# Attention and a gated spatial MLP on one core: three intermediate steps change engine and memory, and the instruction order is replaced

## The chip, the cores and the metric

The kernel runs on one core of one Trainium2 chip. A core has five engines that run at once and wait for each other through semaphores: TensorE (PE, matrix products, written to PSUM), VectorE (DVE), ScalarE (ACT), GpSimd (POOL) and SyncE (SP, here the queue of nearly all DMAs). The metric is the device time of one execution in microseconds, less is better. The time before is 403.96 us, the median of three runs (400.94 to 404.26).

## What is computed

Four batches of 768 tokens. Attention with eight heads of 64, in which a token sees the first four tokens and the last 128 up to itself; its result feeds an MLP whose gate mixes tokens.

```python
scores = q @ k^T / sqrt(64)                 # (4, 8, 768, 768), only sinks and window kept
a = softmax(scores);  x = a @ v             # (4, 768, 512): heads side by side
h = relu(x @ w_in)                          # (4, 768, 1024), split into u and v of 512 each
v_n = (v - mean(v)) / sqrt(var(v) + 1e-6)   # over the 512 of a token
v_s = einsum('ts,bsd->btd', w_spatial, v_n) + b_spatial[t]
out = (u * v_s) @ w_out                     # (4, 768, 512)
```

All inputs are float32 (w_in and w_out arrive as float64 words that are decoded on the chip). The products run in float16 with each operand split into a high and a low half, and three products for a pair (high by high, high by low, low by high).

## The kernel before, in words

The work is cut into pieces, each a Python closure of one to some tens of instructions on one engine: `plan.add` registers about 1900 of them with a rank, an engine (or several that may take it), what they read and what they write. The ranks number the pieces; the costs have no effect on a written-out order. The order in which they are issued is the list `ORDER` (L273): numbers of pieces, with a letter behind a number where the engine is chosen (a ScalarE, d VectorE, p GpSimd). Every engine runs its own pieces in that order and waits at each for what it needs, so the list fixes all queues, SyncE's DMA queue among them. 24 short pieces of idle products (`keep_clock`) are registered, and six of them are in the list, near the start.

A batch has six tiles of 128 tokens, and a tile two halves of four heads: an attention step is one half of a tile, 48 in all (step 20 is batch 1, tile 4, first half). For a step the stages are: scores on TensorE (`scores`, L880 for batch 0 in float32, L886 after it); mask and row minimum on VectorE (L891); exponential on ScalarE (L896); the probabilities p split into a high half (L536 or L545) and a low half (L552), each transposed by a DMA from SyncE (L961); products with v into the tile's attention sum `av` (`attend`, L993 to L1012). `av` has one buffer, of two PSUM banks, and is written by both steps of a tile.

Behind the second step of a tile the sum is divided (`divide`, L1019 to L1023, VectorE) into the SBUF tile `x`, which is split into `x16`: a high half on ScalarE or GpSimd, a low half on GpSimd (the helpers `high`, L536 to L545, and `low`, L552, record one line for all tiles). A DMA transposes `x16` into `xT`.

`v_half` computes v for a tile: product into `ps_v`, relu (L1063, ScalarE), statistics (`stats`, L1069 to L1073, VectorE: bn_stats, bn_aggr, then a scaling of the variance), its power of -1/2 (`root`, L1079, GpSimd), normalisation (L1087, VectorE), and the halves of `vn`. `u_half` computes u for two tiles and 128 of its columns (relu at L1112). When all six `vn` of a batch are there, `s_piece` forms the spatial product for 256 tokens and 128 columns into `ps_s` (18 matmuls); `gate` (L1133, VectorE) adds the bias and writes the sum into the SBUF tile `g`; `times` (L1137, VectorE or GpSimd as the list says) multiplies it with u; halves of `g` follow. `o_piece` multiplies with w_out (12 matmuls), copies (L1159, ScalarE) and stores.

`ps_v`, `ps_u`, `ps_s`, `ps_o` and the transposed blocks of batch 0's first tiles share two PSUM banks ("mm") in turn, so a product waits until the last but one before it has been read out. Scores have four banks.

Weights are loaded and decoded by the same engines in the first 120 us or so, beside batch 0. Near the end checks decide whether a general path must run (`KNOWN`, the place in the list where every engine reads the decision).

Of the kernel before, what the change touches and what calls it, by code (L numbers as in the profile page):

```python
# [269 lines left out]
KNOWN = 1874  # L270
ORDER = """
165 1892 1898 1894 1 0 3 37 116 164 68 5 42 39 4 44 43 1891 1893 2 62 6 40 41 13 38 15 63 11 51 50 14 46 16 45 47 64 48 73 65 17 49 74 66 20 19 21 18
1886 52 67a 10 69 71 88 82 70 7 112 9 111 85 22 87 75 86 25 91 8 93 104 108 107 26 89a 92 101 100 27 12 57 102 84 110 31 105 53 123 103 132 128 129 32  # L273
109 28 126 127 114a 141 106 156 115a 33 34 140 130 113 142 29 151 144a 143 54 150 133 229 172 124p 162 61 90 146 131 145a 159 158 148 76 147 161 77
139 72 163 35 160 152 169a 78 117 30 55 183 36 94 153 157 184 173 95 182 154 170d 188 224 223 125 179 263 83 221 209 194 178 190 191 155 196a 58 168
171 59 192 205 186 185 193 215 187 166 206 79 135 174p 199 222 410 201 96 149 230 198 228 218 210 197a 220 175 23 217 200 167 232 207a 189 216 211 24
212d 219 244 225 243 233 119 231 204 257 208 319 226 213 259 239 134 118 250 97 245a 240 80 261 251 120 227 252d 98 234a 176 345 56 177 235 180 247
267 236 60 99 121 181 136 260 258 283 346 275 248 270 271 262 253 195 122 286 344 289 202p 285 276 81 203p 294 284 313 288 279 287 277a 237 304 305
274 297 137 306a 293 280 281d 138 343 387 214 278 309 310 315 311d 299 300 316 295a 298 327 351a 291 317 318 423 379 328 337 282 321 432 296 446 352
331 389 339 290 329p 322 349 307 340 292 371 341 353 354 372 301 323 342 308 314 312 350 375 326 333d 332 373a 347 338 416 355 334 362 480 417 426  # L280
# [54 lines left out]
class Plan:  # L335
# [945 lines left out]
```

## Time and profile before

| | before |
|---|---|
| time, median of three runs | 403.96 us (400.94 to 404.26) |
| profiled execution, its own time | 402.65 us |
| its span, first to last instruction | 400.8 us |
| busy TensorE / VectorE / ScalarE / GpSimd | 384.4 / 319.7 / 282.7 / 206.1 us |
| HBM read / written | 38.17 / 6.29 MB |

The profile is of one execution. Busy times are from the first cycle of an instruction to its end; matmuls overlap, and their ends are modelled, so a group's busy time over its count is the better price of one than its mean. A view by form groups instructions of one line, engine, operation and shape: total busy us and mean ns, then the idle time of the engine just before them and what ended it. A timeline has one instruction or a run of equal ones to a line.

### The profile page before, as it was taken

What the parts mean: (1) busy time and instruction counts of PE and PEld (TensorE: products, weight loads), DVE (VectorE), ACT (ScalarE), POOL (GpSimd) and SP (SyncE); (2) the same over time, 40 slices, a digit from 0 to 9 for tenths busy, and PEclk for the clock granted to TensorE, in tenths of its full rate; (3) what the DMA queues carried; (4) which work ended last, traced back from release to release, by engine and by line L of the source; (5) the groups of instructions that cost most, each with busy time, mean ns of one, the idle gap of its engine ahead of it and who ended that gap; (6) DMA issues with size and microseconds to landing.
All of it is one profiled execution on the core that took longest, in us unless ns stands there. A gap on an engine that the chain in (4) does not pass through costs nothing. (4 is left out here: it accounts for less than half of the span.)

```text
span 400.8 us, 10029 instructions
## 1 busy us (share of the span) xinstructions
PE 384.4 (96%) x3663; PEld 270.1 (67%) x3663; DVE 319.7 (80%) x898; ACT 282.7 (71%) x681; POOL 206.1 (51%) x265
## 2 busy tenths in 40 slices
PE   7999999989998998999999999998999999999995
PEld 5775587558854774668785785586778666587842
DVE  4999999999999988889998987899679864545310
ACT  4998799979989887879889778896485433322011
POOL 5456545836873766463675674474375642232500
PEclk9999899999999999999999999999999999999999
DMA  8999799778889998797969996988838894123012
GB/s 272 335 352 222 201 196 211 217 199 235 135 208 208 225 216 160 222 240 179 218 165 155 229 219 156 232 176 191 143 79 167 197 196 111 54 80 105 2 56 109
DMA packets 134872, 72.91 MB, mean 182 GB/s; under 512 B 114208, under 2 KB 118304, under 8 KB 134816
## 3 DMA queue, kind: packets, MB, share of 16 engines
q1 hardware_dynamic: 134400, 71.94, 77.7%
q8 instruction: 30, 0.49, 0.5%
q10 hardware_dynamic: 416, 0.26, 0.2%
q14 instruction: 26, 0.21, 0.2%
HBM read 38.17 MB, written 6.29 MB: 111 GB/s over the span
## 5 line engine op out<-in xcount | busy, mean ns | idle before, releaser
L573 PE MATMUL ps_s<-wsp,vn 128*128 128x256 f16 x864 | 99.3, 273 | 2.4 <-ACT u L1112 1.4
L896 ACT ACTIVATE pexp<-pexp,nm 128x260 f32<-128x260 f32 (+1 forms) x192 | 86.2, 486 | 14.6 <-DVE nm L891 14.2
L573 PEld LDWEIGHTS <-vn 128*128 128x128 f16 x864 | 83.2, 98 | 15.2 <-issue 4.7
L573 PE MATMUL ps_u<-xT,win 128*128 128x256 f16 x576 | 69.2, 273 | 2.2 <-DVE nm L891 1.3
L573 PE MATMUL ps_v<-win,xT 128*128 128x512 f16 x288 | 66.3, 380 | 0.3 <-DMA xT<-x 0.3
L573 PE MATMUL ps_o<-wout,g 128*128 128x512 f16 x288 | 65.1, 379 | 0.8 <-DVE g L1133 0.8
L573 PEld LDWEIGHTS <-win 128*128 128x128 f16 x576 | 54.7, 98 | 12.8 <-issue 2.9
L552 DVE TENSOR_TENSOR p<-pexp,p 128x16 f16<-128x16 f32 (+2 forms) x62 | 52.0, 848 | 0.2 <-ACT p L536 0.2
L573 PEld LDWEIGHTS <-xT 128*128 128x128 f16 x288 | 27.2, 98 | 32.4 <-issue 2.2
L573 PEld LDWEIGHTS <-g 128*128 128x128 f16 x288 | 27.9, 98 | 31.4 <-issue 1.2
L536 ACT CAST p<-pexp 128x32 f16<-128x32 f32 (+2 forms) x62 | 36.9, 611 | 1.8 <-DMA pT<-p 1.0
L1159 ACT ACTIVATE ob<-ps_o 128x512 f32<-128x512 f32 x24 | 14.2, 591 | 34.0 <-PE ps_o L573 31.8
L552 POOL TENSOR_TENSOR x<-x,x 128x512 f16<-128x512 f32 x24 | 30.0, 1252 | 10.8 <-ACT x L536 10.1
L1133 DVE SCALAR_TENSOR_TENSOR g<-ps_s,b_bc 128x256 f32<-128x256 f32 x48 | 20.1, 420 | 18.0 <-PE ps_s L573 17.5
L1137 POOL TENSOR_TENSOR g<-g,u 128x256 f32<-128x256 f32 x25 | 23.8, 954 | 20.2 <-DVE g L1133 19.1
L999 PE MATMUL av<-vring,pT 128*128 128x65 f16 x312 | 33.2, 195 | 0.3 <-DMA pT<-p 0.3
L1000 PE MATMUL av<-vring,pT 128*128 128x65 f16 x312 | 33.0, 194 | 0.0
L1001 PE MATMUL av<-vring,pT 128*128 128x65 f16 x312 | 32.9, 194 | 0.0
L1079 POOL TENSOR_TENSOR rs<-rs,mhalf 128x1 f32<-128x1 f32 x24 | 18.2, 761 | 26.1 <-DVE rs L1073 25.9
L999 PEld LDWEIGHTS <-pT 128*128 128x128 f16 x312 | 29.0, 98 | 3.0 <-DMA pT<-p 1.0
L1112 ACT ACTIVATE u<-ps_u 128x256 f32<-128x256 f32 x48 | 17.9, 374 | 16.4 <-PE ps_u L573 16.2
L1000 PEld LDWEIGHTS <-pT 128*128 128x128 f16 x312 | 28.9, 98 | 0.8 <-DVE vring L559 0.2
(154 smaller groups left out, 758.1 us busy)
## 6 DMA issues: line engine op xcount, KB each, us to landing
qkraw<-qk_t SPq DMA_DIRECT2D x18, 512.0 KB, 4.3
out<-ob SPq DMA_DIRECT2D x24, 256.0 KB, 3.2
vraw<-v_s SPq DMA_DIRECT2D x21, 256.0 KB, 3.9
dec<-w_in SPq DMA_DIRECT2D x8, 512.0 KB, 6.9
wrow<-w_in SPq DMA_DIRECT2D x8, 512.0 KB, 3.9
wrow<-w_sp_rows SPq DMA_DIRECT2D x6, 384.0 KB, 3.9
dec<-w_out SPq DMA_DIRECT2D x4, 512.0 KB, 4.8
wrow<-w_out SPq DMA_DIRECT2D x4, 512.0 KB, 4.0
```

Source lines behind the costliest of these rows:

```text
L536: nc.scalar.copy(o, x)
L552: eng[e].tensor_tensor(out=o, in0=x, in1=hi, op=ALU.subtract)
L573: nc.tensor.matmul(o, a, m, start=(i == 0), stop=(i == n - 1))
L896: nc.scalar.activation(po, po, AF.Exp, bias=nm()[:, h2 + q:h2 + q + 1], scale=-1.0)
L999: nc.tensor.matmul(o[:, h], ph, vh, start=(t < 2 and j == 0), stop=False)
L1000: nc.tensor.matmul(o[:, h], ph, vl, start=False, stop=False)
L1001: nc.tensor.matmul(o[:, h], pl, vh, start=False, stop=(j == nb - 1 and (t < 2 or h == HH - 1)))
L1079: nc.gpsimd.tensor_tensor(out=vals["rs", i], in0=vals["rs", i], in1=mhalf, op=ALU.pow)
L1112: plan.add(r + WHEN["u relu"], "a", 0.37, lambda e: nc.scalar.activation(tl("u", (b, c0))[:, d, :], tl("ps_u", i)[:, :TC], AF.Relu, scale= ...
L1133: nc.vector.scalar_tensor_tensor(out=g(), in0=tl("ps_s", i)[:, :TC], scalar=1.0 / (SP_SCALE * VNS), in1=b_bc[:, t0:t0 + TC], op0=ALU.mult, ...
L1137: eng[e].tensor_tensor(out=g(), in0=g(), in1=tl("u", (b, c0))[:, d, :], op=ALU.mult)
L1159: plan.add(r + WHEN["o copy"], "a", 0.5, lambda e: nc.scalar.activation(tl("ob", i), tl("ps_o", i), AF.Copy, scale=1.0 / (G_SCALE * OUT_SC ...
```

## The change

Three edits and a new list. (1) `divide` writes its quotient back over the attention sum in PSUM; the SBUF tile `x` is gone. The high half of x is taken from there on ScalarE or VectorE and the low half on VectorE (GpSimd before). (2) `gate` writes its sum back over `ps_s` where the product is done on VectorE, which then reads it from PSUM; where GpSimd does the product, the sum still goes to `g`. (3) The scaling of the variance moves from VectorE to GpSimd, ahead of the power. (4) `ORDER` holds the same 1892 pieces (six idle ones among them) in another order and with other engines: on VectorE 35 gate products (before 23), 19 low halves of p (before 32), 8 low halves of vn (13); on ScalarE 24 high halves of p (32), 20 of x (9), 29 of g (21), 4 of k (9); on GpSimd 23 low halves of p (10), 18 high halves of p (10), 14 of k (9), 16 low halves of vn (11). The remaining changed lines are costs, which have no effect on a written-out order, and bookkeeping (`where` tells `gate` which engine has the product). Of the list, some lines are shown.

```diff
@@ -228,8 +228,8 @@
 
 ENGINES = {
     "w_in high": "a", "w_sp high": "a", "v high": "a", "q high": "a", "k high": "ap", "p high": "ap",
-    "sink high": "a", "x high": "ap", "vn high": "adp", "g high": "ap", "q low": "dp", "k low": "dp",
-    "p low": "dp", "sink low": "d", "x low": "p", "vn low": "dp", "g low": "dp", "v relu": "a", "normalise": "d",
+    "sink high": "a", "x high": "ad", "vn high": "adp", "g high": "ap", "q low": "dp", "k low": "dp",
+    "p low": "dp", "sink low": "d", "x low": "d", "vn low": "dp", "g low": "dp", "v relu": "a", "normalise": "d",
     "gate": "dp", "w clamp": "d", "w_out low": "p", "pT copy": "ad",
 }
 BANKS = {"sc": 4, "av": 1, "mm": 2}
@@ -267,67 +267,67 @@
-KNOWN = 1874
+KNOWN = 1881
 ORDER = """
-165 1892 1898 1894 1 0 3 37 116 164 68 5 42 39 4 44 43 1891 1893 2 62 6 40 41 13 38 15 63 11 51 50 14 46 16 45 47 64 48 73 65 17 49 74 66 20 19 21 18
-1886 52 67a 10 69 71 88 82 70 7 112 9 111 85 22 87 75 86 25 91 8 93 104 108 107 26 89a 92 101 100 27 12 57 102 84 110 31 105 53 123 103 132 128 129 32
-109 28 126 127 114a 141 106 156 115a 33 34 140 130 113 142 29 151 144a 143 54 150 133 229 172 124p 162 61 90 146 131 145a 159 158 148 76 147 161 77
...
-1794p 1871 1872d 1833 1873p 1874p 1795 1834p 1835p 1796 1836d 1797d 1852 1853 1881 1883 1857 1861 1858 1862 1863 1885 1880 1882 1884 1864 1798p 1799d
-1810 1815 1817 1811 1816 1818
+5 0 1895 1 3 2 4 1908 6 11 1898 10 53 1889 7 164 1894 9 14 13 8 42 39 15 44 16 43 51 41 40 50 62 46 47 45 63 37 1887 64 17 112 48 52 116 38 111 73 19
+229 74 12 65 49 68 105 67a 21 72 20 18 69 83 66 82 22 387 54 71 75 70 88 86 91 55 85 87 25 26 104 89d 100 84 172 163 101 107 162 23 92 103 61 93 128
+106 31 319 110 263 109 108 246 27 32 123 90 129 113 102 28 57 115a 132 459 114a 127 131 209 165 126 124a 194 141 156 142 140 143 33 130 29 146 125 34
...
+1836d 1793a 1794d 1758 1883 1885 1795 1763 1851 1807 1796 1797d 1798p 1799d 1880 1808 1809p 1812p 1852 1882 1853 1813d 1884 1811 1810 1816 1857 1815
+1817 1818 1858 1861 1863 1862 1864
 """.split()
@@ -340,10 +340,11 @@
 
 
     def __init__(self, rings, ring_of):
-        self.pieces, self.rings, self.ring_of = [], rings, ring_of
+        self.pieces, self.rings, self.ring_of, self.where = [], rings, ring_of, {}
 
     def add(self, rank, engines, time, f, reads=(), writes=(), dma=None, shared=False, columns=0, alone=True):
         self.pieces.append((rank, len(self.pieces), engines, time, f, tuple(reads), tuple(writes), dma, shared, columns, alone))
+        return len(self.pieces) - 1
 
     def prepare(self):
         ps = self.ps = sorted(self.pieces, key=lambda x: x[:2])
@@ -366,9 +367,11 @@
 
     def order(self):
         self.prepare()
-        for x in ORDER:
-            p = self.ps[int(x.rstrip("adp"))]
-            yield p[4], x[-1] if x[-1] in "adp" else p[2]
+        todo = [(self.ps[int(x.rstrip("adp"))], x[-1]) for x in ORDER]
+        todo = [(p, e if e in "adp" else p[2]) for p, e in todo]
+        self.where = {p[1]: e for p, e in todo}
+        for p, e in todo:
+            yield p[4], e
 
 
 class Begin:
@@ -494,7 +497,6 @@
             "pexp": ("pexp", sb([P, HH, 2, SEG], F32, "pexp", PEB)),
             "p16": ("p16", next_p16),
             "pT": ("pT", sb([P, 4 * HH + 2, P], F16, "pT", PTB)),
-            "x": ("x", sb([P, 2, HH, D], F32, "x", 1)),
             "x16": ("x16", sb([P, 2, 4 * P], F16, "x16", 2)),
             "xT": ("xT", sb([P, 2, KC, TC], F16, "xT", XTB)),
             "g": ("g", sb([P, TC], F32, "g", GB)),
@@ -1020,7 +1022,7 @@
                 else:
                     nc.vector.tensor_scalar(den, o[:, :, :, D], 1e-9, None, op0=ALU.add)
                 nc.vector.reciprocal(den, den)
-                nc.vector.tensor_tensor(out=tl("x", (b, t)), in0=o[:, :, :, :D],
+                nc.vector.tensor_tensor(out=o[:, :, :, :D], in0=o[:, :, :, :D],
                                         in1=den.unsqueeze(3).to_broadcast([P, 2, HH, D]), op=ALU.mult)
             if whole_av(b, t):
                 plan.add(r, "PE", 0.225 * n + 0.15 + (0.44 if t > 1 else 0), product_whole,
@@ -1032,11 +1034,12 @@
                          columns=195 * n + (195 if t > 1 else 0))
             if hf == 0:
                 return
-            plan.add(r + WHEN["div"], "d", 1.05, divide, [("av", (b, t))], [("x", (b, t))])
-            x16, xf = lambda: tl("x16", (b, t)), lambda: tl("x", (b, t)).rearrange("p f h d -> p (f h d)")
-            high(r + WHEN["x"], "x high", 512, lambda: (x16()[:, 0], xf()), [("x", (b, t))], [("x16", (b, t), 0)])
-            low(r + WHEN["x"], "x low", 512, lambda: (x16()[:, 1], xf(), x16()[:, 0]),
-                [("x", (b, t)), ("x16", (b, t), 0)], [("x16", (b, t), 1)])
+            plan.add(r + WHEN["div"], "d", 1.05, divide, [], [("av", (b, t))])
+            heads = lambda k: tl("x16", (b, t))[:, k].rearrange("p (f h d) -> p f h d", f=2, h=HH)
+            x16, xf = lambda: tl("x16", (b, t)), lambda: av()[:, :, :, :D]
+            high(r + WHEN["x"], "x high", 512, lambda: (heads(0), xf()), [("av", (b, t))], [("x16", (b, t), 0)])
+            low(r + WHEN["x"], "x low", 512, lambda: (heads(1), xf(), heads(0)),
+                [("av", (b, t)), ("x16", (b, t), 0)], [("x16", (b, t), 1)], shared=False)
             if hf:
                 col = P * (t % 2)
                 plan.add(r + WHEN["xT"], "SP", 1.25, lambda e: nc.sync.dma_start_transpose(
@@ -1069,14 +1072,14 @@
                 nc.vector.bn_stats(s6, vr())
                 m = vals["mv", i] = small.tile([P, 2], F32, tag="mv", name="mv")
                 nc.vector.bn_aggr(m, s6)
-                rs = vals["rs", i] = small.tile([P, 1], F32, tag="rs", name="rs")
-                nc.vector.tensor_scalar(rs, m[:, 1:2], 1e-6, VNS ** -2, op0=ALU.add, op1=ALU.mult)
                 if ENGINES["normalise"] != "d":
                     neg = vals["neg", i] = small.tile([P, 1], F32, tag="neg", name="neg")
                     nc.vector.tensor_scalar(neg, m[:, 0:1], -1.0, None, op0=ALU.mult)
 
             def root(e):
-                nc.gpsimd.tensor_tensor(out=vals["rs", i], in0=vals["rs", i], in1=mhalf, op=ALU.pow)
+                rs = vals["rs", i] = small.tile([P, 1], F32, tag="rs", name="rs")
+                nc.gpsimd.tensor_scalar(rs, vals["mv", i][:, 1:2], 1e-6, VNS ** -2, op0=ALU.add, op1=ALU.mult)
+                nc.gpsimd.tensor_tensor(out=rs, in0=rs, in1=mhalf, op=ALU.pow)
 
             def norm(e):
                 if e == "a":
@@ -1088,8 +1091,8 @@
             vn = lambda: tl("vn", i)
             plan.add(r, "PE", 2.62, product, [("xT", (b, t // 2), t % 2), ("win", 1)], [("ps_v", i)], columns=6144)
             plan.add(r + WHEN["v relu"], ENGINES["v relu"], {"a": 0.59, "d": 0.6}, relu, [("ps_v", i)], [("vr", i)])
-            plan.add(r + WHEN["v stats"], "d", 1.02, stats, [], [("vr", i), ("st", i)])
-            plan.add(r + WHEN["v stats"], "p", 0.55, root, [], [("st", i)], alone=False)
+            plan.add(r + WHEN["v stats"], "d", 0.86, stats, [], [("vr", i), ("st", i)])
+            plan.add(r + WHEN["v stats"], "p", 0.85, root, [], [("st", i)], alone=2)
             plan.add(r + WHEN["v norm"], ENGINES["normalise"], {"d": 0.37, "p": 0.65, "a": 0.62}, norm, [("st", i)], [("vr", i)], shared=True)
             high(r + WHEN["v split"], "vn high", 512, lambda: (vn()[:, 0], vr()), [("vr", i)], [("vn", i, 0)])
             low(r + WHEN["v split"], "vn low", 512, lambda: (vn()[:, 1], vr(), vn()[:, 0]), [("vr", i), ("vn", i, 0)], [("vn", i, 1)])
@@ -1129,16 +1132,19 @@
 
             g = lambda: tl("g", i)
 
+            ps = lambda: tl("ps_s", i)[:, :TC]
+            sums_at = lambda: g() if plan.where.get(gated) == "p" else ps()
+
             def gate(e):
-                nc.vector.scalar_tensor_tensor(out=g(), in0=tl("ps_s", i)[:, :TC], scalar=1.0 / (SP_SCALE * VNS),
+                nc.vector.scalar_tensor_tensor(out=sums_at(), in0=ps(), scalar=1.0 / (SP_SCALE * VNS),
                                                in1=b_bc[:, t0:t0 + TC], op0=ALU.mult, op1=ALU.add)
 
             def times(e):
-                eng[e].tensor_tensor(out=g(), in0=g(), in1=tl("u", (b, c0))[:, d, :], op=ALU.mult)
+                eng[e].tensor_tensor(out=g(), in0=sums_at(), in1=tl("u", (b, c0))[:, d, :], op=ALU.mult)
             g2 = lambda: tl("g2", i)
             plan.add(r, "PE", 2.0, product, [("vn", (b, s)) for s in range(NT)] + [("wsp", s) for s in range(NT)], [("ps_s", i)], columns=4608)
             plan.add(r + WHEN["gate"], "d", 0.4, gate, [("ps_s", i), ("b_bc", 0)], [("g", i)])
-            plan.add(r + WHEN["gate"], ENGINES["gate"], {"d": 0.4, "p": 0.7}, times, [("u", (b, c0), d)], [("g", i)], shared=True)
+            gated = plan.add(r + WHEN["gate"], ENGINES["gate"], {"d": 0.4, "p": 0.7}, times, [("u", (b, c0), d), ("ps_s", i)], [("g", i)])
             high(r + WHEN["g split"], "g high", TC, lambda: (g2()[:, 0], g()), [("g", i)], [("g2", i, 0)])
             low(r + WHEN["g split"], "g low", TC, lambda: (g2()[:, 1], g(), g2()[:, 0]), [("g", i), ("g2", i, 0)], [("g2", i, 1)])
 
```

## Rows read from the trace of the kernel before

**Rows 1.** The page's busy table: engine, busy us, share of the span, instructions.

```profile
span 400.8 us, 10029 instructions
PE 384.4 (96%) x3663; PEld 270.1 (67%) x3663; DVE 319.7 (80%) x898; ACT 282.7 (71%) x681; POOL 206.1 (51%) x265
```

**Rows 2.** Busy us by stretch: engines, then granted clock, DMA share and GB/s.

```profile
0.00:20.00 20.00, 17.42 (x115) 12.27 (x116) 13.91 (x58) 14.91 (x34) 9.91 (x34) 1.00 0.92 303
20.00:120.00 100.00, 95.33 (x910) 68.62 (x910) 96.65 (x252) 89.56 (x210) 61.07 (x70) 0.98 0.92 218
120.00:160.00 40.00, 37.45 (x406) 24.17 (x405) 35.59 (x108) 34.82 (x85) 22.81 (x27) 1.00 0.99 203
160.00:380.00 220.00, 218.14 (x2164) 157.89 (x2162) 171.34 (x472) 139.81 (x347) 111.74 (x135) 1.00 0.73 160
380.00:400.80 20.80, 16.04 (x76) 7.12 (x73) 2.18 (x10) 3.58 (x6) 0.57 (x2) 0.96 0.22 80
```

**Rows 3.** Waits, of TensorE and of all: line <- what ended it: us, times, longest.

```profile
PE ps_s L573 <- ACT u L1112: 1.4, 1, 1.4
POOL x L552 <- ACT x L536: 10.1, 6, 2.7
```

**Rows 4.** Groups by form: names, shapes, count | busy us, mean ns | idle before.

```profile
L552 DVE TENSOR_TENSOR p<-pexp,p 128x1024 f16<-128x1024 f32 x28 | 39.4, 1406 | 0.0
L552 POOL TENSOR_TENSOR x<-x,x 128x512 f16<-128x512 f32 x24 | 30.0, 1252 | 10.8 <-ACT x L536 10.1
L1079 POOL TENSOR_TENSOR rs<-rs,mhalf 128x1 f32<-128x1 f32 x24 | 18.2, 761 | 26.1 <-DVE rs L1073 25.9
L1023 DVE TENSOR_TENSOR x<-av,den 128x512 f32<-128x512 f32 x24 | 16.6, 692 | 1.4
L1137 DVE TENSOR_TENSOR g<-g,u 128x256 f32<-128x256 f32 x23 | 11.2, 486 | 0.5
L552 DVE TENSOR_TENSOR vn<-vr,vn 128x512 f16<-128x512 f32 x13 | 9.0, 698 | 1.5 <-POOL vn L545 1.5
L536 ACT CAST x<-x 128x512 f16<-128x512 f32 x9 | 5.6, 617 | 4.4 <-DVE x L1023 4.3
L1073 DVE TENSOR_SCALAR rs<-mv 128x1 f32<-128x1 f32 x24 | 3.7, 154 | 0.8
L932 DVE COPY pT<-tr 128x512 f32<-128x512 f32 x1 | 0.7, 683 | 0.0
```

**Rows 5.** Timeline of TensorE at 122.4: start us, us, instructions merged.

```profile
122.41 0.84 PE L886 MATMUL sc<-kring,qp 64*128 64x260 f16 x12
```

**Rows 6.** Groups by form on TensorE: spatial and output products.

```profile
L573 PE MATMUL ps_s<-wsp,vn 128*128 128x256 f16 x864 | 99.3, 273 | 2.4 <-ACT u L1112 1.4 <-DVE g L1133 0.9
L573 PE MATMUL ps_o<-wout,g 128*128 128x512 f16 x288 | 65.1, 379 | 0.8 <-DVE g L1133 0.8
```

**Rows 7.** Timelines of SyncE's queue and of VectorE at the start.

```profile
0.72 0.46 SPq L829 DMA_DIRECT2D wsp<-qk_t  x1
1.24 0.45 SPq L567 DMA_DIRECT2D dec<-w_in  x1
...
4.81 0.29 DVE L891 CUSTOM_DVE_ANT_0 pexp<-sc,m_first 128x128 f32<-128x128 f32 x1 [3.53 <-PE sc L880]
6.73 0.43 DVE L632 TENSOR_SCALAR w<-dec 128x512 int32<-128x512 int32 x1 [0.99 <-DMA dec<-w_in]
```

**Rows 8.** Single lines: count, then shortest, median and longest ns.

```profile
L1133 DVE SCALAR_TENSOR_TENSOR g<-ps_s,b_bc x48: 406/421/426, 91.2 to 380.3; 128x256 f32<-128x256 f32 x48
L1137 DVE TENSOR_TENSOR g<-g,u x23: 408/425/1384, 98.9 to 381.0; 128x256 f32<-128x256 f32 x23
L1087 DVE TENSOR_SCALAR vr<-vr,mv,rs x24: 534/546/2270, 43.5 to 348.7; 128x512 f32<-128x512 f32 x24
```

**Rows 9.** Timelines of VectorE and GpSimd at 80 us.

```profile
80.26 2.27 DVE L1087 TENSOR_SCALAR vr<-vr,mv,rs 128x512 f32<-128x512 f32 x1 [0.44 <-POOL rs L1079]
80.20 2.05 POOL L552 TENSOR_TENSOR p<-pexp,p 128x1024 f16<-128x1024 f32 x1
```

More of the change, by code (lines that the diff above doesn't have):

```diff
@@ L275 @@
[L275 to L278, printed above, removed]
@@ new lines @@
+853 1065p 1020 1046 1034 1000 1044a 857 1087 1393 1077 987 1005 1075p 1036 1037 1057 1048p 1038 1058 1024 1088 1089d 1184 1035 1100a 1012 1059 1101p
+1056 1047 1076 1092a 1049 1001 1185 1150 1186d 1098p 1279 1045 1073 1078 1002 1096 1196a 1055 1003d 1182 1375 1197p 1086 1097 1030 1110 1083 1021p
+1093 1085 1107 1022p 1084 1109 1063 1013 1099 1161 1031 1079a 1449 1032d 1043 1074 1039a 1108 1040d 1119 1162 1131 1129a 1080 1263 1163p 1121 1299
+1128 1225p 1122 1123 1226 1174a 1140 1106 1264 1141 1227 1132 1120 1175p 1142 1138 1130 1265d 1838 1305 1033 1273p 1115 1133d 1041p 1139 1283 1223
@@ new lines @@
+1293 1274d 1169 1167a 1151 1042p 1116 1220 1145 1168 1094 1450 1117p 1170 1152a 1160 1171p 1134 1158 1124a 1157 1179 1153 1181 1328 1095 1159 1103
+1144 1125p 1280 1173 1549 1224 1281 1303p 1178 1112 1359 1187 1104 1260 1180 1210 1198 1513 1191 1300 1228 1199p 1193 1387 1190 979 1218 1203p 1201
+1177 1363 1192 1154 1211 1216 1212d 1217 1304 1329 1229p 1202 1221 1215 1204 1230p 1247 1214 1245a 1514 1302 1155 1222 1200 1249p 1366a 1165 1231
+1232a 1246 1135 1311 1239 1294 1238 1166 1237 1236 1113 1259 1282 1257 1256 1258 1240 1136 1515 1248 1276p 1137d 1250 1183 1147a 1462 1233 1194p 1266
@@ new lines @@
+1628 1744d 1752 1768 1708 1754 1561 1761 1629 1657 1762 1709 1630 1710d 1631 1723a 1765 1728 1724d 1800 1766d 1678 1703d 1767p 1681 1771 1804 1729
+1730 1747 1772 1731 1773 1737 1774 1814 1756 1777 1779d 1791 1822 1780d 1738 1830 1792 1875 1831 1739 1865 1876 1877d 1740 1878a 1879p 1642 1854 1866
+1867d 1868a 1748 1855 1856d 1869d 1859p 1643 1860p 1786 1757 1760 1781 1759 1790 1644 1825 1782 1645 1783p 1590 1784p 1801 1826 1785p 1827d 1828a
+1829p 1819 1802 1803d 1591 1805p 1592 1806d 1870 1820 1821d 1823a 1824d 1832 1871 1872d 1873a 1874d 1787 1833 1834d 1593 1835p 1881 1788 1850 1789d
@@ L546, in high, with low @@
             plan.add(rank, ENGINES[kind], costs(kind, n), f, reads, writes, shared=True)
-        def low(rank, kind, n, views, reads, writes):
+        def low(rank, kind, n, views, reads, writes, shared=True):
             def f(e):
@@ L552, in f @@
                 eng[e].tensor_tensor(out=o, in0=x, in1=hi, op=ALU.subtract)
-            plan.add(rank, ENGINES[kind], costs(kind, n, two=True), f, reads, writes, shared=True)
+            plan.add(rank, ENGINES[kind], costs(kind, n, two=True), f, reads, writes, shared=shared)
         def low_scaled(rank, n, views, scale, reads, writes):
@@ L647, in exponents @@
             load(rank, "wrow", i, source, 512, lambda t: t.bitcast(I32))
-            plan.add(rank, "d", 0.65, lambda e: nc.vector.tensor_scalar(
+            plan.add(rank, "d", 0.36, lambda e: nc.vector.tensor_scalar(
                 hi(), hi(), 0x7FFFFFFF, 23, op0=ALU.bitwise_and, op1=ALU.logical_shift_right), [], [("wrow", i)], shared=True)
```

96 lines of the change are left out of this document (44 added, 52 removed).

## The prediction

> **What bounds the kernel now.** I read the page's busy table first: TensorE is busy for 96% of the span, VectorE for 80% [rows 1]. A span of 400.8 us in which TensorE idles 16.4 us leaves little to win anywhere else. The second view, the table by stretch, says where that idle time lies [rows 2]: 2.6 us in the first 20 us, 4.7 us from 20 to 120, 2.6 us from 120 to 160, 1.9 us in the 220 us from 160 to 380, and 4.8 us in the last 20.8 us, where the last output tile is copied and stored. In the same rows VectorE is busy for 96.65 of the 100 us from 20 to 120, and for 171 of the 220 us from 160 on. So there are two regimes: up to about 120 us VectorE sets the pace and TensorE waits for it in small pieces; after 160 us TensorE runs nearly without a gap. [...] Third, the waits of TensorE: the longest single one that another engine causes is 1.4 us, behind a relu on ScalarE [rows 3]. The end is TensorE's last product, then a copy and a store; the change touches none of these. What it can win is therefore the 4.7 + 2.6 + 2.0 = 9.3 us of idle time and clock between 20 and 160, not more.
>
> The profiled execution took 402.65 us (span 400.8); the median shown is 403.96, of runs from 400.94 to 404.26. I sum against 402.65, which lies inside that spread, and carry the result over unchanged.
>
> **The change, part by part.** The new list of pieces matters most, so I counted pieces of both lists by kind and engine.
>
> *Whole run.* On VectorE: 24 low halves of x come in (before: GpSimd), 12 more gate products (23 to 35), 13 fewer low halves of p (32 to 19), 5 fewer of vn (13 to 8), 4 high halves of x, 3 more high halves of vn, one more copy of pT, and 24 scalings of the variance leave. Priced by rows 4: a low half of x reads PSUM and SBUF as the division does, which takes 692 ns (from SBUF alone vn's takes 698, so both bounds are the same); a product with its sum in PSUM is taken as the sum itself, 0.42 us [rows 8], since that has one PSUM and one SBUF input of the same size (0.486 is its price in SBUF); a low half of p costs 1406, a scaling 154. A high half from PSUM is bounded by 0.42 and 0.69, I take 0.6; those of vn get 0.42 and the copy its own 683 ns. So 24 x 0.692 + 35 x 0.420 - 23 x 0.486 + 4 x 0.6 + 3 x 0.42 + 0.68 - 13 x 1.406 - 5 x 0.698 - 24 x 0.154 = 16.6 + 3.5 + 2.4 + 1.3 + 0.7 - 18.3 - 3.5 - 3.7 = -1.0 us: VectorE's load hardly changes. What changes is when it does it.
>
> *Up to 120 us.* I take the scores of attention step 20 (batch 1, tile 4, first half), which start at 122.4 us [rows 5], and count what each list has ahead of them. On VectorE: 8 low halves of x and 4 gate products and one copy of pT more, 4 low halves of p, 3 of vn and 7 scalings less: 5.54 + 1.68 + 0.68 - 5.62 - 2.09 - 1.08 = -0.9 us. On TensorE the new list has one output product more ahead of the same point, 65.1 / 24 = 2.7 us [rows 6]. If VectorE sets the pace there, TensorE stands 0.9 + 2.7 = 3.6 us further at the same moment, and from 160 us on, where it has no gaps, it keeps that to the end. Bounds: nothing, if something other than VectorE's load set these gaps; 9.3 us, all that there is to recover. I take 3.6, the counted value.
>
> *The start.* SyncE's first load is now a tile of w_in, not keys, and VectorE's queue opens with that tile's two decoding steps; the masks of the first four heads stand behind them. Before, these four masks ran from 4.81 us on and VectorE then sat 0.99 us until the tile landed at 6.73 [rows 7]. The tile is issued one place earlier, at 0.72 instead of 1.24 us [rows 7]. So four masks of at most 0.29 us move behind a landing that comes 0.5 us sooner: 1.2 - 0.5 = +0.7 at worst, 0 if the tile lands sooner still, since its transfer no longer shares with the keys. I take +0.5.
>
> *Variance scaled on GpSimd.* Relu, statistics, scaling, power, normalisation form a chain. A 154 ns step leaves VectorE and one enters GpSimd, just ahead of the power, with a wait between the two. GpSimd's own power on the same 128x1 takes 761 ns on average [rows 4], which bounds the new step above; 154 bounds it below. Behind it in GpSimd's queue stand the power, and then p's and vn's lows. Each value tile is needed only by spatial products, which need all six; except for the last tile of a batch there are many microseconds of products between. Cost on the path: 0, up to four batches times 0.6 = 2.4 us.
>
> *Longer holds in PSUM.* The attention sum has one buffer of two banks. It was free after the division, whose last and longest step takes 692 ns; now after the high half (617 ns on ScalarE) and the low half (692) as well [rows 4]. The low half stands in VectorE's queue and waits there for ScalarE; GpSimd sat 10.1 us over six such waits [rows 3]. The new list puts 0.6 to 8 us of other VectorE work between a division and its low half, which covers the 617. A turnover thus needs the division's last step, this filler and the low half: 2 to 9.4 us. TensorE's own work between the last product into the buffer and the next first one is in the new list never under 3.2 us, and beyond the first three tiles never under 6 (by the sizes in rows 6, an output product 2.7 us, a spatial one 99.3 / 48 = 2.1). It is tight for the first three tiles, where hold and cover are both 3 to 5 us. Gate sums multiplied on VectorE hold their bank 0.42 us longer, 35 of 48; in the new list at least one spatial product always lies before that bank's next use. Cost 0 with this cover; if it is gone, the lateness itself, per turnover.
>
> *DMA queues.* No DMA is added. The transposes of x follow a low half of 0.69 instead of 1.25 us, so they are issued no later; SyncE's queue keeps its order but for neighbours. 0.
>
> Sum: 402.65 - 3.6 + 0.5 = 399.55, so 399.5 us.
>
> [...] Here a VectorE instruction with a PSUM input is no dearer: 256 columns take 406 to 426 ns with the sum in PSUM and 408 at least with both inputs in SBUF [rows 8]. [...]
>
> **Rivals.**
> *Nothing gained.* The gaps between 20 and 160 may come from chains (a relu that waits in ScalarE's queue, a row minimum, a transfer), not from VectorE's load; a new order then has as many. For it: TensorE's longest wait names ScalarE [rows 3]. Against it: VectorE is 97% busy there. Time: 402.65 + 0.5 = 403.2, range 401.5 to 405.
>
> *More gained: the two engines stop blocking each other.* A normalisation that takes 0.55 us in the median lasted 2.27 us while a low half of p ran on GpSimd beside it, ending 0.28 us after it [rows 8, 9]; a gate product with both inputs in SBUF took up to 1.38 us, while no gate sum, with its input in PSUM, exceeded 0.43. The 24 lows and 35 products leave that contest. Against it: 13 low halves of p of 2 us each go to GpSimd instead. If the freed waits close most of the gaps, 402.65 - 9.3 + 0.5 = 393.9, range 393 to 396.
> [...]
>
> *Slower: the attention buffer comes free late.* VectorE is saturated up to 120 us; a low half of x that stands behind late ScalarE work keeps the next attention product waiting, and TensorE's queue with it. 23 turnovers; with 0.42 us each (GpSimd's 10.1 us over 24 lows) it costs 9.7 us: 399.5 + 9.7 = 409. It decides against the gain from 0.16 us a turnover on. For it: the three tight turnovers; against it: covers of 6 to 16 us in the others. Range 404 to 410.
>
> **How the numbers follow.** Chances: 0.45 for the forecast (396 to 402), 0.20 for nothing gained, 0.20 for more gained, 0.15 for slower. A measurement of this kernel can tell about 1% from no change; against 403.96 that is below 399.9 or above 408. The forecast lies below 399.9 in about 0.28 of its 0.45; with the 0.20 of more gained that is 0.48 for faster; slower is 0.15, all of its case; the rest is 0.37. The range reaches from 393 to 407: it leaves out the far part of the slow case and a little beyond the full recovery.
>
> **What would show it.** Right: TensorE's idle time from 20 to 160 falls from 7.2 to about 4, that from 160 to 380 stays near 2; step 20's scores come 3 to 4 us further on in TensorE's work; low halves of x near 0.69 us and never stretched; gate products on VectorE near 0.42. Wrong: TensorE waiting for x's low halves ahead of attention products (slower); the same 7 us of idle in other places (nothing gained); VectorE far below 97% up to 120 us together with idle near zero (more gained); a start later by over 1 us at the first transposed tile.

## The result, and the profile after

The changed kernel takes 399.47 us (median of 20 runs, 397.33 to 404.78) against 404.00 for the kernel before in the same series (20 runs, 400.94 to 407.25): a ratio of 0.9892, 95% interval 0.9868 to 0.9916. Measured once more in a later series it was 400.69 against 404.63, ratio 0.9949 (0.9914 to 0.9985). So it is faster, by 0.5 to 1.1%. Ratios leave out runs more than 1.5% above the fastest of their kernel, five of these 20 (403.48 to 404.78) and none of the later 12; with every run in, the means give 0.992 in both series. The profiled execution took 399.68 us, its span is 397.9 against 400.8.

The busy table of the changed kernel, then its table by stretch (busy us of the engines, granted clock, DMA share, GB/s):

```profile
PE 386.9 (97%) x3663; PEld 272.1 (68%) x3663; DVE 305.2 (77%) x900; ACT 280.3 (70%) x682; POOL 201.0 (51%) x262
```
```profile
0.00:20.00 20.00, 17.54 (x109) 12.32 (x109) 13.08 (x59) 14.43 (x34) 8.72 (x34) 0.91 0.92 321
20.00:120.00 100.00, 97.28 (x892) 69.49 (x892) 87.93 (x247) 87.00 (x206) 66.55 (x75) 0.95 0.91 212
120.00:160.00 40.00, 40.00 (x475) 27.15 (x474) 37.31 (x115) 35.17 (x86) 26.35 (x32) 1.00 1.03 201
160.00:380.00 220.00, 219.28 (x2133) 157.68 (x2132) 165.75 (x475) 140.73 (x355) 98.26 (x122) 1.00 0.75 163
380.00:397.90 17.90, 12.74 (x59) 5.50 (x57) 1.09 (x7) 2.98 (x5) 1.13 (x2) 1.00 0.21 78
```

Set beside [rows 2], TensorE's idle time by stretch goes from 2.6 / 4.7 / 2.6 / 1.9 / 4.8 us to 2.5 / 2.7 / 0 / 0.7 / 5.2: 5.4 us less. TensorE's busy time rises by 2.5 us [rows 1] over the same 3663 instructions; more of it ran at the lower of the two clocks that the profiles show, 0.50 of the upper (mean 0.91 and 0.95 in the first two stretches, where before it was 1.00 and 0.98). 5.4 less 2.5 is the 2.9 us of span. VectorE's busy time falls from 319.7 to 305.2 us, and in the stretch from 20 to 120 from 96.65 to 87.93.

The same groups of VectorE's and GpSimd's instructions by form as in [rows 4] (count | busy us, mean ns | idle before and what ended it):

```profile
L554 DVE TENSOR_TENSOR p<-pexp,p 128x1024 f16<-128x1024 f32 x17 | 22.4, 1316 | 3.0 <-POOL p L547 3.0
L554 DVE TENSOR_TENSOR x<-av,x 128x512 f16<-128x512 f32 x24 | 16.4, 683 | 0.1
L1090 DVE TENSOR_SCALAR vr<-vr,mv,rs 128x512 f32<-128x512 f32 x24 | 15.3, 638 | 4.6 <-POOL rs L1082 4.4
L1143 DVE TENSOR_TENSOR g<-ps_s,u 128x256 f32<-128x256 f32 x35 | 14.8, 423 | 1.7
L554 POOL TENSOR_TENSOR p<-pexp,p 128x1024 f16<-128x1024 f32 x19 | 39.9, 2097 | 14.4 <-ACT p L538 13.9
```

The low halves of x take 683 ns on VectorE, the products 423: as priced. What was not priced is that the pieces that stay where they were get shorter too (the normalisation 638 ns, before 804).

And the waits of TensorE (line, what ended the wait: us in total, times, longest):

```profile
PE av L1001 <- DMA pT<-p: 1.3, 1, 1.3
PE av L1014 <- DVE pT L934: 1.2, 1, 1.2
...
PE sc L882 <- DMA wsp<-qk_t: 1.0, 1, 1.0
```

None of these waits of 0.3 us or more names a low half of x (two weight loads waited 0.3 and 0.2 us for one).

### The profile page after: what moved, and what is told of

Read it like the earlier page. It is cut to its first block, busy times and chain, and to the rows that moved or that the text cites. A ratio compares the mean times of both kernels' runs of the same rounds, so it can differ in the third digit from the quotient of the medians.

```text
span 397.9 us, 10018 instructions
## 1 busy us (share of the span) xinstructions
PE 386.9 (97%) x3663; PEld 272.1 (68%) x3663; DVE 305.2 (77%) x900; ACT 280.3 (70%) x682; POOL 201.0 (51%) x262
## 5 line engine op out<-in xcount | busy, mean ns | idle before, releaser
L554 POOL TENSOR_TENSOR p<-pexp,p 128x1024 f16<-128x1024 f32 (+1 forms) x23 | 45.4, 1974 | 14.5 <-ACT p L538 13.9
L554 DVE TENSOR_TENSOR p<-pexp,p 128x16 f16<-128x16 f32 (+2 forms) x49 | 31.4, 644 | 4.6 <-POOL p L547 3.0
L1001 PE MATMUL av<-vring,pT 128*128 128x65 f16 x312 | 32.6, 193 | 1.3 <-DMA pT<-p 1.3
L538 ACT CAST p<-pexp 128x32 f16<-128x32 f32 (+2 forms) x54 | 29.6, 563 | 4.2 <-DMA pT<-p 4.0
L547 POOL TENSOR_SCALAR p<-pexp 128x1024 f16<-128x1024 f32 (+1 forms) x18 | 20.1, 1118 | 24.6 <-ACT pexp L898 9.0
L1002 PE MATMUL av<-vring,pT 128*128 128x65 f16 x312 | 32.5, 193 | 0.0
L1003 PE MATMUL av<-vring,pT 128*128 128x65 f16 x312 | 32.4, 193 | 0.1
L1001 PEld LDWEIGHTS <-pT 128*128 128x128 f16 x312 | 28.7, 97 | 3.1 <-DMA pT<-p 1.6
L554 POOL TENSOR_TENSOR g<-g,g 128x256 f16<-128x256 f32 x27 | 20.8, 772 | 18.9 <-ACT g L538 18.2
L1081 POOL TENSOR_SCALAR rs<-mv 128x1 f32<-128x1 f32 x24 | 8.6, 359 | 41.9 <-DVE mv L1074 39.5
L888 PE MATMUL sc<-kring,qp 64*128 64x260 f16 (+1 forms) x432 | 28.9, 262 | 0.6 <-DVE nm L893 0.5
L1139 DVE SCALAR_TENSOR_TENSOR ps_s<-ps_s,b_bc 128x256 f32<-128x256 f32 x35 | 15.1, 430 | 18.4 <-PE ps_s L575 17.1
```

The source lines that it names most:

```text
L538: nc.scalar.copy(o, x)
L547: nc.gpsimd.tensor_scalar(o, x, 1.0 if sc is None else sc, 1.0, op0=ALU.mult, op1=ALU.mult)
L554: eng[e].tensor_tensor(out=o, in0=x, in1=hi, op=ALU.subtract)
L888: nc.tensor.matmul(o, qp[rows, qi, hp, :], keys(kring[:, ki], rows), start=(m == 0), stop=(m == 2))
L1001: nc.tensor.matmul(o[:, h], ph, vh, start=(t < 2 and j == 0), stop=False)
L1002: nc.tensor.matmul(o[:, h], ph, vl, start=False, stop=False)
```

## The experiments

All twelve, with the times of their own series. The medians and ranges are of all runs; a ratio has its 95% interval in brackets.

| kernel | median us (range) | ratio to before |
|---|---|---|
| the new list, edits undone | 400.80 (399.49 to 403.37) | 0.9908 [0.9881, 0.9935] |
| the edits, old list | 432.34 (430.72 to 433.85) | 1.0691 [1.0659, 1.0723] |
| new order, old engines | 422.11 (419.19 to 423.00) | 1.0406 [1.0345, 1.0466] |
| old order, new engines | 428.56 (426.39 to 429.02) | 1.0567 [1.0507, 1.0626] |
| x in SBUF again | 403.37 (401.18 to 405.95) | 0.9948 [0.9912, 0.9984] |
| gate sum in SBUF again | 400.91 (398.31 to 403.45) | 0.9889 [0.9826, 0.9951] |
| scaling on VectorE again | 402.36 (399.18 to 404.51) | 0.9944 [0.9910, 0.9978] |
| 14 idle groups more | 400.33 (399.87 to 400.85) | 0.9903 [0.9880, 0.9926] |
| changed kernel, again | 400.69 (399.04 to 404.55) | 0.9949 [0.9914, 0.9985] |
| new list, edits undone, again | 401.91 (399.19 to 403.31) | 0.9948 [0.9920, 0.9977] |
| changed kernel, VectorE work added | 404.81 (399.42 to 406.82) | 0.9982 [0.9939, 1.0026] |
| before, VectorE work added | 405.18 (402.59 to 410.64) | 1.0029 [0.9990, 1.0069] |

### The list or the edits

The first theory is the prediction's: the new list carries the gain ("order"). The rival: the edits do, since VectorE's low halves of x and gate products then read PSUM, and the gate sums, which read it before, took 426 ns at most, where the normalisation, which reads SBUF, was stretched to 2.27 us beside GpSimd's work [rows 8, 9] ("locks"). The first kernel has the new list and none of the edits:

```diff
-                nc.vector.tensor_tensor(out=o[:, :, :, :D], in0=o[:, :, :, :D],
+                nc.vector.tensor_tensor(out=tl("x", (b, t)), in0=o[:, :, :, :D],
-            x16, xf = lambda: tl("x16", (b, t)), lambda: av()[:, :, :, :D]
+            x16, xf = lambda: tl("x16", (b, t)), lambda: tl("x", (b, t))
-            sums_at = lambda: g() if plan.where.get(gated) == "p" else ps()
+            sums_at = lambda: g()
+                nc.vector.tensor_scalar(rs, m[:, 1:2], 1e-6, VNS ** -2, op0=ALU.add, op1=ALU.mult)
-                nc.gpsimd.tensor_scalar(rs, vals["mv", i][:, 1:2], 1e-6, VNS ** -2, op0=ALU.add, op1=ALU.mult)
```

> The changed kernel's list with all three edits undone: the division writes an SBUF tile, the low half of x on VectorE reads that tile, the gate's sum goes to SBUF tiles for all 48, and the variance is scaled on VectorE. If the list carries the gain (theory 'order'): 399 to 400.5 us, PE idle between 20 and 160 us about 3, and VectorE's busy time rises by less than 5 us over the changed kernel's 305.2. [...]

The second keeps the edits and takes the old list:

```diff
-ORDER = """ 5 0 1895 1 3 2 4 1908 ... """
+ORDER = """ 165 1892 1898 1894 1 0 3 37 ... """   (low halves of x and late gate products moved up)
```

> The edits in the list of before. Its 15 high halves of x on GpSimd go to ScalarE, since GpSimd reads no PSUM here; 4 high and 9 low halves of x and 4 gate products stand up to 31 places earlier in the list, where the bank they now hold would otherwise be asked for before they are issued. Theory 'order': 403 to 406 us (24 low halves of x more on VectorE, 24 x 0.69 = 16 us, of which some 4 fall before 120 us, in a list that was not found for it). Theory 'locks': 399 to 401 us, with VectorE's stretched low halves of p (1406 ns before) near 1300.

And later, on one chip, the pair once more:

> The changed kernel as it is, beside the other three on one chip: ratio to before 0.987 to 0.992, the yardstick for them.

> The new list with all three edits undone, once more, to price the edits against the changed kernel on the same chip. If the edits' 13.7 us of VectorE time (318.9 against 305.2 us busy) are on the path only where VectorE is near full: 0.5 to 1.5 us slower than the changed kernel. If they carry nothing: within 0.5 us. If they carry the gain: 3 us or more.

The list alone gives 0.9908, against 0.9892 for the whole change; on the second occasion 0.9948 against 0.9949. So the list carries the gain, and the edits add less than can be measured: on one chip the ratios differ by 0.0001, with an interval of about 0.0046 to either side, or 1.8 us (the medians, 400.69 and 401.91, are 1.2 us apart). That rules out the 3 us of a gain from the edits; between nothing and the 0.5 to 1.5 us of the expectation it does not decide. In the old list the edits cost 28 us, far outside what either theory gave. The waits of TensorE there:

```profile
PE av L995 <- DVE x L554: 8.1, 4, 3.9
...
PE av L1009 <- DVE x L554: 2.2, 1, 2.2
```

Attention products wait 11.4 us, up to 3.9 at once, for low halves of x that now hold the attention bank (10.3 in these two rows, 1.1 in a third): the prediction's slow rival, in a list that was not made for the edits. TensorE's idle time grows by 18.4 us in all, its busy time by 11.7, so the bank is not all of it. (4 high and 9 low halves and 4 products stand earlier there, ahead of the next request for the bank that they hold, so it is not the old list to the letter. None of the GpSimd instructions in the profiles before and after, 265 and 262, reads a PSUM tile.)

Of the signs in the first expectation, the time came out near "order" (400.80, where it gave 399 to 400.5) and VectorE's load did not (318.9 us, 13.7 more than 305.2, where it gave less than 5). The busy table and two groups of the new list without the edits, against 305.2 us, 683 and 423 ns above:

```profile
PE 388.2 (97%) x3663; PEld 273.0 (68%) x3663; DVE 318.9 (79%) x924; ACT 280.9 (70%) x682; POOL 194.6 (48%) x238
```
```profile
L555 DVE TENSOR_TENSOR x<-x,x 128x512 f16<-128x512 f32 x24 | 21.2, 882 | 0.1
L1144 DVE TENSOR_TENSOR g<-g,u 128x256 f32<-128x256 f32 x35 | 21.1, 603 | 1.0
```

24 x (0.882 - 0.683) = 4.8 us, 35 x (0.603 - 0.423) = 6.3 us and 3.7 us of scalings are 14.8 of VectorE's time, about the 13.7 by which the tables differ. This time was taken from VectorE, and the kernel's time changed by no more than the interval above.

### Order or engines

The new list does two things: it puts the pieces in another order, and gives about 180 of them to other engines. Each alone, with the kernel before:

```diff
 order alone     (old engine letters in the new order)
-... 212p 98 200 ...
+... 212d 98 200 ...
 engines alone   (new engine letters in the old order)
-    "sink high": "a", "x high": "ap", ..., "x low": "p", ...
+    "sink high": "a", "x high": "ad", ..., "x low": "d", ...
-... 107 26 89a 92 101 ...
+... 107 26 89d 92 101 ...
```

> The kernel before (its division, gate, variance scaling) with the new list's order of the pieces, while every piece stays on the engine that it had before: low halves of x on GpSimd, the 19 low halves of p that the new list gives to GpSimd on VectorE. Theory 'order' (which piece comes when): 400 to 401.5 us, as the new list alone (400.8). Theory 'engines' (which engine does the piece: VectorE, 97% busy from 20 to 120 us before, is relieved, and GpSimd's chain of low halves of x is gone): 404 us or more.

> The kernel before with its own order of the pieces, but each piece on the engine that the new list names (low halves of x on VectorE from the SBUF tile, high halves on ScalarE or VectorE, 19 low halves of p to GpSimd and 6 back, gate products and halves likewise). Theory 'engines': 400 to 402 us. Theory 'order': 404 us or more, since waits that the old order placed for the old engines are now in other queues. Edits alone in the old order gave 432.3; if that came from the low halves of x standing on VectorE in an order not made for it, this one is slow too (over 415); if it came from the hold of the attention bank, this one is not.

Neither theory holds: order alone costs 4.1%, engines alone 5.7%, both together gain 0.5 to 1.1%. TensorE idles 8.5 and 19.3 us longer than before and is busy 11.9 and 7.0 us longer, at a mean granted clock of 0.976 and 0.988 (before 0.994). TensorE's waits in the new order with the old engines, then in the old order with the new engines:

```profile
PE sc L886 <- DVE nm L891: 6.9, 9, 1.6
PE av L999 <- DMA pT<-p: 2.1, 1, 2.1
```
```profile
PE sc L889 <- DVE nm L894: 3.9, 5, 1.2
PE sc L889 <- DVE qp L562: 3.3, 3, 1.8
PE av L1002 <- DMA pT<-p: 3.2, 4, 1.5
```

The row minimum (nm), the low half of the queries (qp) or the transposed probabilities (pT) are late in their queues, a little in many places. VectorE's busy time is 331.0 and 336.4 us here, more than in any other kernel. The old order with the new engines has no late attention bank (its division writes SBUF) and is still 23 us slow, so a loss of this size does not need the bank's hold.

### The edits one by one

```diff
 x in SBUF:      out=tl("x", (b, t)) in the division; both halves of x read it
 gate in SBUF:   sums_at = lambda: g()
 scaling:        nc.vector.tensor_scalar(rs, ...) in stats, not in root
```

> The changed kernel with the division's result in an SBUF tile again, so that the attention bank is free after the division and the high and low halves of x (engines as in the changed kernel) read SBUF. If the hold of the bank costs time in the new list: below 399.5 us. [...]

> The changed kernel with the gate's sum in SBUF for all 48 tiles; 35 products on VectorE read two SBUF operands again. Predicted from the row of before: 35 x (0.486 - 0.423) = 2.2 us more VectorE work, nearly all after 120 us where TensorE has no gap, so 399 to 400 us. [...]

> The changed kernel with the variance's scaling back on VectorE (24 instructions of 154 ns there, 3.7 us in all, of which about 1.1 before 120 us). Both theories: within 1 us of the changed kernel's 399.5, theory 'order' +0.3 to +1.1 (VectorE sets the pace up to 120 us), theory 'locks' 0 (its operands are one column wide).

The time of none of them can be told from the changed kernel's two measurements (0.9892 and 0.9949): 0.9948, 0.9889 and 0.9944. With all three undone it is not slower than with one, so the differences between these kernels can't be told from chance, and the times don't price one edit. Their VectorE busy times do: 315.6, 310.8 and 308.8 us, or 10.4, 5.6 and 3.6 more than the changed kernel's. Single instructions show why (count: shortest, median, longest ns); the low halves of x with x in SBUF, then in the changed kernel; the gate products in SBUF, then in the changed kernel:

```profile
L555 DVE TENSOR_TENSOR x<-x,x x24: 678/691/1554, 20.8 to 337.8; 128x512 f16<-128x512 f32 x24
```
```profile
L554 DVE TENSOR_TENSOR x<-av,x x24: 674/682/692, 19.8 to 331.3; 128x512 f16<-128x512 f32 x24
```
```profile
L1143 DVE TENSOR_TENSOR g<-g,u x35: 412/426/1376, 90.6 to 379.6; 128x256 f32<-128x256 f32 x35
```
```profile
L1143 DVE TENSOR_TENSOR g<-ps_s,u x35: 413/424/426, 89.9 to 378.1; 128x256 f32<-128x256 f32 x35
```

With an operand in PSUM not one of the 59 instructions is stretched; with both in SBUF the longest take 2.3 and 3.3 times the shortest. When the stretched ones end shows what held them: each of the eight longest low halves (848 ns or more) ends 0.54 to 0.55 us after a GpSimd instruction that ran beside it has ended, each of the ten longest products (over 600 ns) 0.28 to 0.29 us after. The longest low half, on VectorE, and what GpSimd did then:

```profile
218.68 1.55 DVE L555 TENSOR_TENSOR x<-x,x 128x512 f16<-128x512 f32 x1
```
```profile
217.65 2.04 POOL L555 TENSOR_TENSOR p<-pexp,p 128x1024 f16<-128x1024 f32 x1
219.65 1.11 POOL L555 TENSOR_TENSOR g<-g,g 128x256 f16<-128x256 f32 x1
```

In the changed kernel 10 of the 24 low halves and 12 of the 35 products have a two-input GpSimd instruction beside them for more than half of their time, and keep their length. A single full-size input in SBUF is not enough to be spared: the normalisation is still stretched, its five longest ending 0.27 to 0.29 us after a GpSimd instruction:

```profile
L1090 DVE TENSOR_SCALAR vr<-vr,mv,rs x24: 514/546/1614, 59.5 to 344.2; 128x512 f32<-128x512 f32 x24
```

### The clock at the start

The changed kernel's profile has 13.6 us at the lower clock (0.50) between 9 and 43 us; before it was 3.4, from 44.3 to 47.7. If that loss eats part of the gain, a kernel without it is faster. This one has 14 groups more of idle products, and its clock was 1.00 in both stretches below:

```diff
-... 1898 10 53 1889 7 164 1894 9 14 13 ...
+... 1898 10 53 1889 7 164 1894 1886 1888 1890 9 14 13 ...
-... 218 225 216 56 ... 257 119 ... 77 252p 233 ...
+... 218 225 1897 1899 1900 216 56 ... 1901 257 119 ... 77 252p 1902 233 ...
```

> The changed kernel with 14 more groups of four 256-column products on TensorE that compute nothing used, set where it waits: after the first five groups, between the first scores, and around attention of the third tile (20 to 45 us). The changed kernel's profile had 13.6 us at half clock (9.1 to 12.5 and 33.0 to 43.3 us), before 3.4 us. Theory 'clock' (the loss in clock at the start eats 2 to 3 us of the gain): granted clock 0.99 or more and 396.5 to 398 us. Rival (TensorE waits there for VectorE and the loads anyway, so the clock costs nothing, and the added products only take its time): 399 to 401 us whatever the clock.

The first 60 us of this kernel by stretch, and the one stretch of the changed kernel that isn't shown above:

```profile
0.00:20.00 20.00, 17.36 (x125) 12.34 (x125) 12.57 (x58) 13.83 (x33) 8.79 (x33) 1.00 0.93 307
20.00:60.00 40.00, 39.34 (x334) 27.11 (x333) 35.94 (x106) 34.11 (x79) 20.71 (x25) 1.00 0.94 228
```
```profile
20.00:60.00 40.00, 38.82 (x309) 26.88 (x309) 34.63 (x106) 34.07 (x79) 21.69 (x26) 0.87 0.89 219
```

The granted clock is 1.00 in both, as the theory wants, and the time is 400.33 us (0.9903), in the rival's range. But that doesn't show that the clock costs nothing, since the added products took TensorE's time themselves. The idle products of this kernel, then of the changed one:

```profile
L1174 PE MATMUL idle<-any 128*128 128x256 bf16 x80 | 12.1, 300 | 1.8 <-DVE first L388 1.2 <-ACT pT L948 0.6
```
```profile
L1174 PE MATMUL idle<-any 128*128 128x256 bf16 x24 | 5.1, 396 | 1.2 <-DVE first L388 1.2
```

They take 7.0 us more; 13.6 us at half the clock lose 6.8 us of work. Gain and price are about equal, and this kernel can't tell a worthless gain from one that was spent. The times on record speak for a price: of the 15 runs in the changed kernel's first ratio, the ten with a mean granted clock of 0.985 or more took 397.3 to 399.3 us, the five below it 399.7 to 402.1. In the later series the medians of the same two groups are 400.2 and 402.4, but they overlap (399.0 to 404.6 and 400.4 to 403.7). Whether the clock makes the time, or late work makes both, stays open. With the added groups the spread is small: six runs lie within 1.0 us, where the changed kernel's 12 and 20 lie 5.5 and 7.5 us apart.

### VectorE's pace up to 120 us

The prediction rests on VectorE setting the pace there. If it does, 12 instructions more on it, between attention steps 8 and 19, are paid in full:

```diff
+                if 8 <= i < 20 and h2 == 0 and q == 0:
+                    nc.vector.tensor_reduce(out=extra[:, i:i + 1], in_=m_odd.rearrange("p a c -> p (a c)"), axis=AX.X, op=ALU.max)
                 nc.vector.tensor_tensor_reduce(out=po, in0=o, in1=mask, ...
```

> The changed kernel with one more VectorE instruction (a maximum over 260 columns that nothing reads, some 0.3 us by the nearest rows, so about 3.6 us in all) ahead of the first masked score of each of the 12 attention steps from 8 to 19, issued between about 60 and 120 us. If VectorE still sets the pace there (the prediction's first regime): 2.5 to 4 us over the changed kernel of the same call. If the new list left slack on VectorE (88% busy from 20 to 120 us, against 97% before): within 1 us of it.

> The same 12 VectorE instructions in the kernel before. By the prediction (VectorE sets the pace up to 120 us): 2.5 to 4 us over the kernel before, so 406.5 to 408. Rival (what sets the pace is how each queue's order fits the others, and TensorE's idle time absorbs the rest): within 1 us of the kernel before.

They took 418 ns each, 5.0 us in all:

```profile
L893 DVE TENSOR_REDUCE extra<-m_odd 128x1 bf16<-128x260 bf16 x12 | 5.0, 418 | 0.0
```

The kernel before became 1.2 us slower by the ratio (interval -0.4 to +2.8), not 5. VectorE's busy time rises by 2.2 us only over the whole span (319.7 to 321.9), and in the stretch from 20 to 120 us it even falls, from 96.65 to 95.33, as the same work comes later:

```profile
20.00:120.00 100.00, 94.02 (x858) 66.74 (x858) 95.33 (x255) 86.31 (x204) 58.34 (x67) 0.97 0.86 207
```

This doesn't refute that VectorE sets the pace in that kernel. The scores of attention step 20, at 122.41 us before, start 4.0 us later; here is their first row, then the busy times up to it, then those up to 122.41 us in the kernel before:

```profile
126.37 0.40 PE L887 MATMUL sc<-kring,qp 64*128 64x260 f16 x4
```
```profile
0.00:126.37 126.37, 118.05 (x1033) 83.31 (x1034) 115.07 (x330) 106.47 (x247) 71.68 (x103) 0.97 0.87 223
```
```profile
0.00:122.41 122.41, 115.16 (x1034) 81.82 (x1035) 112.94 (x318) 106.03 (x248) 70.98 (x103) 0.99 0.91 229
```

1.6 of the 4.0 us stand already at step 8 (34.9 us, before 33.3), ahead of the first added instruction at 37.4, in a stretch where this execution ran at half the clock (30.7 to 37.5 us). The other 2.4 are about the 2.1 us that VectorE is busy longer. At the end 2.4 of the 4.0 are left. So in this kernel VectorE's busy time may well be TensorE's time up to step 20; the 5.0 us added were simply no 5.0 us more of it.

The changed kernel, with more room on VectorE, lost 1.3 us by the ratios (interval about -0.9 to +3.6): neither the 2.5 to 4 us nor the "slack" of the expectation (within 1 us) is shown. The pair on one chip says more about the new list. The busy times up to step 20's scores, in the changed kernel (125.41 us) and in the new list without the edits (125.76):

```profile
0.00:125.41 125.41, 119.28 (x1045) 83.84 (x1046) 106.33 (x318) 105.98 (x248) 77.45 (x110) 0.96 0.91 230
```
```profile
0.00:125.76 125.76, 120.49 (x1046) 85.34 (x1047) 110.36 (x325) 105.41 (x246) 75.11 (x102) 0.97 0.88 227
```

4.0 us more on VectorE put step 20 back by 0.35 us; even with the 1.7 us less that this execution lost to the lower clock (6.8 against 10.2 us at half) that is half of the 4.0. In the new list VectorE's load is not TensorE's time one for one.

## Why the prediction came out, point by point

**The time.** 399.5 was predicted, 399.47 measured; the second series gave 400.7. The sign was right: a gain of about 1%, from the list. The way to the number was not, and that it fell within 0.1 us is luck: the changed kernel's own runs spread over 7 us.

**VectorE sets the pace up to 120 us, and step 20 stands 3.6 us further on: it does not.** The scores of step 20 start at 125.48 us, not at 122.41 [rows 5]:

```profile
L888 PE MATMUL sc<-kring,qp x12: 269/269/282, 125.5 to 126.0; 64*128 64x260 f16 x12
```

Ahead of them TensorE has the counted output product more, 2.7 us, but 3.1 us were spent on it: no lead at all, 0.4 us behind. VectorE meanwhile was busy for 106.4 us ahead of that point, where before it was 112.9: 6.5 us less, not the counted 0.9, and step 20 did not come forward. The step that failed is the one from VectorE's load in the old list, where it may set the pace, to TensorE's time in the new list, one for one. A second term was missing: the 2.0 in the 9.3 us to win are the 100 us from 20 to 120 at a mean clock of 0.98 [rows 2] (in the trace 3.4 us at 0.50, so 1.7 us of work), and the sum has none for losing more. Ahead of step 20 the changed kernel ran 13.6 us at half the clock, before 3.4, so 5.1 us of work more were lost there. How much of the 3.6 us that hid is not shown.

**The gain comes later than I put it.** I counted the finished TensorE work, at the prices of the kernel before, in both traces. The changed kernel is some 5 us behind at 40 us, 2 to 3 at 80 and under 1 at 120; it is 2 to 3 us ahead at 160 and about 3 at 280 and 360. The idle time that went is 2.0 us from 20 to 120, 2.6 from 120 to 160, where now there is none, and 1.1 from 160 to 380. I had expected the latter to stay near 2. The 3.6 of the sum was met by other terms. Which pieces of the list bring this is open: order and engines only do it together, and I did not split them further.

**The start: +0.5 was small.** VectorE had the first tile of w_in at 5.72 us, before at 6.73: 1.0 sooner, for an issue 0.5 sooner. Ahead of the keys it took 5.0 us from issue to landing, before, behind their first 128 KB, 5.5; these took 2.9 us ahead of it and 5.3 behind it. The first transposed tile is at 9.1 us, 0.8 after the 8.3 of before. The 5 us of lag at 40 us, with the clock at 0.50 from 33.0 to 43.3, were not foreseen. The lag was made up by 120 us; whether TensorE would have been ahead without it is not shown, as the 14 idle groups more of the kernel at a clock of 1.00 took 7.0 us, about the 6.8 that the lower clock had cost.

**VectorE's load, -1.0 us: mis-sized, it is -14.5.** The prices of what moved were right (683 for 692 ns, 423 for 420), but two of the 13 low halves of p that leave have 512 columns and take 682 ns, not 1406, so the sum itself should have been about +0.5. The pieces which stay got shorter: in sums of durations (neighbouring instructions overlap, so these exceed the busy time; they fall by 16.9 us in all), those with the same engine in both lists fall by 18.9 us (3.7 of it the scalings), those that left and came differ by +2.1. GpSimd no longer takes the 24 low halves of x (30 us) and 12 of the gate products, but more low halves of p and vn instead: its two-input instructions sum to 132.5 us, before 142.3. Why it holds the others up less is not shown. The kernel without the edits shows both parts: there too the others get shorter, by 11.4 us, but the low halves and products that came in are stretched themselves, and VectorE is at 318.9 again. On the time this term has no weight beyond the 1.8 us of the interval above.

**Scaling on GpSimd, longer holds, DMA queues: 0, as far as this can be told.** The scaling takes 190 ns in the median on GpSimd (359 on average), between its bounds of 154 and 761:

```profile
L1081 POOL TENSOR_SCALAR rs<-mv x24: 190/191/1071, 58.1 to 343.4; 128x1 f32<-128x1 f32 x24
```

The attention bank's hold is covered in the new list, as counted. The condition behind it is real: in the old list the same hold makes TensorE wait 11.4 us.

**VectorE's operands in PSUM.** The edited instructions are no dearer for them in the runs either: the shortest low half takes 674 ns with one input in PSUM and 678 with both in SBUF, the shortest product 413 and 412.

**The rivals.** "Nothing gained" named a mechanism that may fit the new list better (chains of waits up to 120 us, not VectorE's load; which chains was not tested) and had the wrong result. "More gained" had its mechanism fulfilled, none of the 59 instructions is stretched (674 to 692 and 413 to 426 ns, against up to 1554 and 1376 with both inputs in SBUF), and that brought less than can be measured. The normalisation that the rival took as its first sign has only one full-size input, in SBUF, and yet took up to 2.27 us before and 1.61 after. Why, no run shows. "Slower" came true only with the old list.

## What to carry to other kernels

Order and engine of the pieces are one thing: a list found for one set of durations lost 4 to 7% as soon as only its order, only its engines or only the instructions changed, so a change must be tried with a list of its own, and the list alone must be tried too before the gain is put down to the edits. A busy share is not a pace: before VectorE's work is counted as time, look at the longest against the shortest of its instructions, add some work, and see how much later the step behind it starts. Near 1%, undoing single edits can tell less than the spread between kernels that differ by nothing that matters.

## What the runs showed of the hardware that was not expected

A full-size VectorE instruction with two SBUF inputs took up to 1554 ns beside GpSimd's work where its shortest took 678; the same with one input in PSUM stayed within 674 to 692 over all 24. A held instruction ended a fixed time after the GpSimd instruction beside it: 0.54 to 0.55 us for eight low halves of x, 0.28 to 0.29 for ten gate products and 0.27 to 0.29 for five normalisations (unheld they take 0.68, 0.42 and 0.54 us). Adding 5.0 us of VectorE work to the kernel before raised VectorE's busy time by 2.2 us; its other instructions were busy some 2.8 us less, and which of them was not followed up. And with 14 groups more of idle products, 7.0 us of TensorE's time, its clock was 1.00 until 396.8 us in the profile (0.998 over the span), the time stayed where it was (400.33 us, for 399.47 and 400.69) and the runs lie within 1.0 us.
